# Sparse attention and a gated MLP on one core: K and Q loaded in runs of six tokens by casting transfers, with a newly searched instruction order

## The chip, the cores and the metric

The kernel runs on one core of a Trainium2 chip. The metric is the device time of one execution in microseconds (us); a kernel's time is the median of several executions. The profiler records one execution, whose span is some 1.8 us shorter than the time of the same execution. A run is called slow when it is over 1.5% above the fastest run of the same kernel, otherwise fast. Wherever a ratio of two kernels is given, it is the mean time of one kernel's fast runs over the mean time of the other's fast runs of the same rounds on the same chip, so it is not quite the ratio of the medians quoted beside it. For most runs it is found again only if the profiled execution is left out.

The engines are named as in the profile: PE (TensorE), PEld (its weight loads), DVE (VectorE), ACT (ScalarE), POOL (GpSimd) and SP (SyncE, which here only issues transfers).

## The reference

Attention over 4 batches, 8 heads, 768 tokens and head size 64, with the BigBird mask (window, first and last block, three random blocks of 32 tokens), feeds a gated MLP with a spatial gate and a residual.

```python
scores = scale * np.matmul(q, k.transpose(0, 1, 3, 2))     # (4, 8, 768, 768)
mask = |blk_i - blk_j| <= 1, or block 0 or 23 on either side, or one of 3 random blocks per row
attn = softmax(where(mask, scores, -1e9))
x = (attn @ v) as (batch, 768, 8 * 64)

h = gelu_tanh(x @ w_in)                                     # 512 -> 1024
u, v = h[..., :512], h[..., 512:]
v_n = layernorm(v) * g_ln
v_s = einsum('ts,bsd->btd', w_sg, v_n) + b_sg               # 768 x 768 over tokens
out = x + (u * v_s) @ w_out
```

The inputs are float32. The kernel does the attention products in bfloat16.

## The kernel before

The program is a list of operations, each with an engine, its dependencies, a modelled duration and a priority. Before anything is emitted, a greedy model of the chip turns the list into one fixed order per engine. Each engine then executes its list strictly in that order, with semaphores for the dependencies. So priorities and modelled durations do not change what is computed; they change who stands in front of whom.

```python
# in schedule(): the order is made on modelled times
for o in self.ops:
    o.prio = -rk[o.idx] if RANK == 1 else o.prio - RANK * rk[o.idx]
...  # greedy: the engine with the earliest possible start takes its best candidate
c = min((c for c in cands if c[0] <= tmin + 0.03), key=lambda c: (c[1], c[2]))
```

TensorE needs K and Q with the head dimension on the partitions, so every pair of heads is loaded with tokens on partitions, cast to bfloat16, transposed on TensorE into PSUM, and copied ("evicted") from PSUM to the tiles `KT` and `QT`. For batches 1 to 3 this went through two staging buffers, shared with V:

```python
ST = sb("ST", [P, 2, 768], F32)                    # the ring: two buffers of 384 KB
...
# one load of two heads on the SP queue; a run is one token of one head, 64 floats = 256 B
sr = SRC[nm][b, 2*c:2*c+2].rearrange("h (t p) d -> p (h t) d", p=P)
ld = op("SP", f"ld{nm}{b}.{c}", lambda e: e.dma_start(sg, sr), w=[sk], ...)
# then a cast, on GpSimd for K and Q of batches 1 to 3
op(eng, f"cs{nm}{b}.{c}", fn, r=[sk], w=w, dur={"DVE": 0.6, "ACT": 0.85, "POOL": 1.0}[eng], prio=pr)
...
# six transposes per pair of heads, both heads in one stationary operand
for t in range(T):
    ins = pe.transpose(Mbf[:, cc:cc + P], n_[:, c, t, :], ident[:, :])
...
# eviction: contiguous for batches 1 to 3, K on DVE, Q on ACT
src = Mbf[:, u.slot*1024:u.slot*1024 + S]
o_ = TT[:, c, 0:S]
if b == 0:     # batch 0 is loaded two tokens per run, and evicted with a strided write
    src = src.rearrange("p (n j c) -> p n j c", n=3, j=2)
    o_ = o_.rearrange("p (n c j) -> p n j c", n=3, j=2)
```

V has a path of its own, which the change leaves alone except in the order: staged and cast the same way, written to a scratch area in device memory (`scr`), and read back by gathers (`VG`, `VS`, `VR`), some of them indirect ones on GpSimd.

The softmax here doesn't subtract the row's maximum and nothing guards it: scores larger than these inputs give would overflow.

## Time and profile before

| | |
|---|---|
| time, median of the first three runs | 286.02 us (284.76 to 287.4) |
| span of the profiled execution | 280.6 us (timed at 282.39 us, so a quick one) |
| TensorE busy, idle | 216.9 us, 63.7 us |
| packets, of them under 512 B | 93,852, 68,468 |
| GpSimd waiting for K and Q loads | 50.7 us |

From the page of the kernel before: first the busy time of each engine with its share of the span and its instructions; then the busy tenths in 40 slices of 7 us; then the packets, and for each queue its packets, megabytes and share of the time of 16 transfer engines.

```profile
span 280.6 us, 8680 instructions
...
PE 216.9 (77%) x3525; PEld 159.9 (57%) x3525; DVE 163.8 (58%) x469; ACT 152.4 (54%) x227; POOL 112.4 (40%) x208
...
PE   0134675878776999974588998969669999999974
...
DMA  8999989999969768588996794868910112320033
...
DMA packets 93852, 45.43 MB, mean 162 GB/s; under 512 B 68468, under 2 KB 88084, under 8 KB 93812
...
q1 hardware_dynamic: 86848, 34.26, 54.5%
q0 software_dynamic: 4128, 9.02, 12.8%
```

TensorE is the busiest engine, but it has 64 us of holes, and the transfer engines are full for the first 80 us. Most packets are small. Queue 1 is the SP queue, with the staged loads; queue 0 holds the transfers that GpSimd issues.

The waits view of the kernel before (who waited for whom, us in total, times, longest):

```profile
POOL kn L559 <- DMA ST<-in_k_dram: 34.7, 9, 9.5
...
POOL qn L559 <- DMA ST<-in_q_dram: 16.0, 7, 4.9
...
PE Mps L591 <- POOL qn L559: 13.0, 8, 3.0
...
PE Mps L591 <- POOL kn L559: 1.8, 2, 1.2
```

GpSimd, whose casts stand in order with its gathers, waits 50.7 us for staged K and Q data, and TensorE then waits 14.8 us for those casts. The chain of waits that ended last (start, duration, what) shows the ring of two buffers at work:

```profile
55.61 5.42 DMA ST<-in_k_dram
61.08 0.83 POOL kn L559
61.93 3.59 SPq L548
65.56 11.65 DMA scr<-VA
...
133.10 4.07 DMA ST<-in_q_dram
...
197.53 7.19 DMA ST<-in_q_dram
```

A load lands, a cast frees its buffer, and only then the SP queue can go on: its next issue takes 3.6 us, and behind it the write of V to scratch takes 11.7 us to issue and land. The groups of the K and Q path, by line, engine and tile (count, then busy us and mean ns, then idle before them):

```profile
L559 POOL CAST kn<-ST 128x768 bf16<-128x768 f32 x12 | 10.0, 830 | 34.7 <-DMA ST<-in_k_dram 34.7
...
L591 PE MATMUL Mps<-ident,kn 128*128 128x128 bf16 x96 | 9.4, 254 | 13.7 <-ACT kn L559 9.2 <-DVE x_tok L898 2.3 <-POOL kn L559 1.8
...
L604 DVE COPY KT<-Mps 128x768 bf16<-128x768 bf16 x12 | 6.4, 551 | 8.4 <-PE Mps L591 8.2
```

And three of the stretches of 20 us (stretch, length, then busy us of PE, PEld, DVE, ACT and POOL with their instructions, the granted TensorE clock, the share of the transfer engines, GB/s):

```profile
100.00:120.00 20.00, 20.00 (x512) 15.38 (x513) 12.52 (x36) 14.63 (x23) 8.13 (x17) 1.00 0.68 154
120.00:140.00 20.00, 11.39 (x179) 8.20 (x172) 10.28 (x37) 7.83 (x11) 9.38 (x11) 0.88 0.87 222
...
200.00:220.00 20.00, 15.46 (x126) 12.00 (x128) 10.28 (x28) 10.75 (x18) 10.48 (x23) 0.83 0.20 47
```

The stretches 120 to 140 and 200 to 220 us are where the next batch's K and Q arrive late.

### The profile page before, as it was taken

To read this page: it belongs to the slowest core of one execution; us is meant where nothing else is said; L and a number is where in the kernel's file an instruction comes from. 1 tells how busy PE (TensorE), PEld (TensorE's weight loads), DVE (VectorE), ACT (ScalarE), POOL (GpSimd) and SP (SyncE) were. 2 spreads that over 40 slices of the span, in tenths; PEclk is the share of its full clock that TensorE was granted. 3 is DMA by queue.
4 is the path that set the end of the run, shared out by engine and by line. 5 is a ranking of instruction groups with operands and counts; after the bars stand their busy time and mean duration, and the time that the engine had idled before them with its cause. 6 is when DMAs were issued, how large, how long until landed. Compare 5 with 4: busy or idle time off the path is not lost.

```text
span 280.6 us, 8680 instructions
## 1 busy us (share of the span) xinstructions
PE 216.9 (77%) x3525; PEld 159.9 (57%) x3525; DVE 163.8 (58%) x469; ACT 152.4 (54%) x227; POOL 112.4 (40%) x208
## 2 busy tenths in 40 slices
PE   0134675878776999974588998969669999999974
PEld 0123454766454677762466676756467777868442
DVE  6108634212986658529254897655934685557783
ACT  3471876845064657750556756745527667766000
POOL 1017863160387865125669543128674220012000
PEclk9999998779999999999689999997959999999999
DMA  8999989999969768588996794868910112320033
GB/s 155 245 279 220 231 189 283 270 204 235 263 116 238 165 148 185 130 208 214 248 208 154 143 211 100 202 165 218 265 31 3 31 45 56 127 66 0 0 114 112
DMA packets 93852, 45.43 MB, mean 162 GB/s; under 512 B 68468, under 2 KB 88084, under 8 KB 93812
## 3 DMA queue, kind: packets, MB, share of 16 engines
q1 hardware_dynamic: 86848, 34.26, 54.5%
q0 software_dynamic: 4128, 9.02, 12.8%
q10 hardware_dynamic: 2836, 1.60, 2.7%
q8 instruction: 28, 0.46, 0.7%
q14 instruction: 12, 0.10, 0.1%
HBM read 36.49 MB, written 9.55 MB: 164 GB/s over the span
## 4 chain that ended last, share of the span: by engine, by line
PE 40%; DMA 19%; SPq 12%; POOL 11%; issue 10%; DVE 5%; ACT 2%; POOLq 0%
PE Mps L394 25%; DMA ST<-in_q_dram 7%; PE Ops L394 6%; POOL VR L678 6%; PE Sps L394 5%; SPq L548 5%; DMA ST<-in_k_dram 5%; DMA scr<-VA 4%; SPq L670 3%; DMA uT<-in_k_dram 3%; DVE gt L979 2%; SPq L632 2%; POOL KR L695 2%; PE Mps L913 2%; POOL qn L559 2%
## 5 line engine op out<-in xcount | busy, mean ns | idle before, releaser
L678 POOL DMA_INDIRECT VR<-scr,IDX x47 | 46.4, 987 | 24.0 <-issue 9.0
L691 DVE COPY KR<-KT 128x128 bf16 x176 | 33.2, 256 | 9.1 <-PE Sps L394 4.7
L394 PE MATMUL Mps<-w_sgT,vh 128*128 128x384 bf16 x192 | 35.1, 327 | 0.2
L695 POOL COPY KR<-KT 128x128 bf16 x88 | 23.5, 308 | 21.2 <-PE Sps L394 21.1
L394 PE MATMUL Mps<-w_out,xg 128*128 128x512 f32 x96 | 29.5, 433 | 1.9 <-DVE xg L982 1.6
L394 PE MATMUL Mps<-w_in,xg 128*128 128x512 f32 x96 | 27.5, 432 | 3.1 <-ACT vg L937 2.1
L979 DVE SCALAR_TENSOR_TENSOR gt<-Mps,gcol,bsg 128x384 f32<-128x384 f32 x32 | 19.7, 617 | 16.2 <-PE Mps L394 15.6
L394 PE MATMUL Mps<-xg,w_in 128*128 128x384 f32 x128 | 28.3, 368 | 0.7 <-ACT uT L964 0.2
L770 ACT ACTIVATE PR<-Sps 96x1024 bf16<-96x1024 f32 (+1 forms) x24 | 22.8, 948 | 8.2 <-PE Sps L394 8.2
L997 DVE TENSOR_TENSOR x_tok<-Mps,x_tok 128x512 f32<-128x512 f32 x24 | 16.6, 690 | 16.3 <-PE Mps L394 16.0
L394 PEld LDWEIGHTS Mps<-xg,w_in 128*128 128x128 f32 x128 | 22.9, 202 | 4.4 <-ACT uT L964 1.8
L937 ACT ACTIVATE vg<-Mps 128x512 f32<-128x512 f32 x24 | 14.2, 597 | 20.0 <-PE Mps L394 18.4
L604 ACT ACTIVATE QT<-Mps 128x768 bf16<-128x768 bf16 x14 | 11.6, 839 | 23.3 <-PE Mps L591 15.3
L394 PEld LDWEIGHTS Mps<-w_sgT,vh 128*128 128x128 bf16 x192 | 17.2, 98 | 11.9 <-DVE gt L979 1.4
L559 POOL CAST kn<-ST 128x768 bf16<-128x768 f32 x12 | 10.0, 830 | 34.7 <-DMA ST<-in_k_dram 34.7
L591 PE MATMUL Mps<-ident,qn 128*128 128x128 bf16 x96 | 9.9, 252 | 17.7 <-POOL qn L559 13.0
L394 PEld LDWEIGHTS Mps<-w_in,xg 128*128 128x128 f32 x96 | 18.0, 202 | 9.0 <-ACT vg L937 3.6
L920 ACT ACTIVATE xg<-Mps 128x512 fp32r<-128x512 f32 x24 | 14.3, 594 | 15.5 <-PE Mps L913 15.3
L394 PEld LDWEIGHTS Mps<-w_out,xg 128*128 128x128 f32 x96 | 17.1, 196 | 7.3 <-DVE xg L982 2.4
L950 DVE TENSOR_SCALAR vh<-vg,lnmv,lny 128x512 bf16<-128x512 f32 x24 | 13.3, 594 | 13.2 <-POOL lny L946 13.2
L964 ACT ACTIVATE uT<-Mps 128x384 f32<-128x384 f32 x32 | 15.7, 492 | 9.7 <-PE Mps L394 9.3
L939 DVE BATCH_NORM_STATS2 lnst<-vg 128x6 f32<-128x512 f32 x24 | 16.3, 679 | 7.8 <-ACT vg L937 7.8
(98 smaller groups left out, 399.7 us busy)
## 6 DMA issues: line engine op xcount, KB each, us to landing
out_dram<-x_tok SPq DMA_DIRECT2D x20, 256.0 KB, 3.4
ST<-in_v_dram SPq DMA_DIRECT2D x12, 384.0 KB
ST<-in_k_dram SPq DMA_DIRECT2D x12, 384.0 KB
ST<-in_q_dram SPq DMA_DIRECT2D x12, 384.0 KB
VR<-scr SPq DMA_DIRECT2D x123, 32.5 KB, 2.9
scr<-VA SPq DMA_DIRECT2D x6, 390.0 KB, 6.9
w_in<-in_moe_w_in_dram POOLq DMA_DIRECT2D x1, 2048.0 KB, 9.6
VS<-scr SPq DMA_DIRECT2D x3, 650.0 KB, 7.5
```

The costliest lines, as they stand in the source:

```text
L394: return pe.matmul(o, l, r, start=start, stop=True, skip_group_check=True)
L559: fn = {"DVE": lambda x: x.tensor_copy(o4, i4), "ACT": lambda a: a.activation(o4, i4, ACT.Copy), "POOL": lambda g: g.tensor_copy(o4, i4)}[eng]
L678: return g.indirect_dma_start(out=VR[0:96, uV.slot, :, :].rearrange("p h e -> p (h e)"), out_offset=None, in_=src[:, :], in_offset=bass.In ...
L691: ins = x.tensor_copy(KR[:, c0:c0 + n, rg, 32 * j:32 * j + 32], KT[:, c0:c0 + n, bass.ds(vals["DVE", i][j][0], 32)])
L695: op("POOL", f"kp{b}.{i}{hh}", lambda x, i=i, rg=rg: x.tensor_copy(KR[:, c0:c0 + n, rg, 64:96], KT[:, c0:c0 + n, bass.ds(vals["POOL"][0][i ...
L770: return lambda a: a.activation(o, i_, ACT.Exp, scale=SCALE)
L920: return x.tensor_copy(o_, i_) if xe == "DVE" else x.activation(o_, i_, ACT.Copy)
L937: op("ACT", f"gV{b}.{tau}", lambda a: a.activation(vg[vr][:, :], Mps[:, u.slot * 512:u.slot * 512 + 512], ACT.Gelu_apprx_tanh), r=[("vp", ...
L939: op("DVE", f"bs{b}.{tau}", lambda x: x.bn_stats(lnst[:, vr, :], vg[vr][:, :]), r=[("vg", vr)], w=[("lnst", vr)], dur=0.73, prio=pr - 300)
L964: o = op("ACT", f"gU{b}.{c}{dt}", lambda a: a.activation(uT[c][:, dt, :], Mps[:, u.slot * 512:u.slot * 512 + 384], ACT.Gelu_apprx_tanh), r ...
L979: op("DVE", f"g1{b}.{c}{dt}", lambda x: x.scalar_tensor_tensor(gt[gr][:, :], Mps[:, u.slot * 512:u.slot * 512 + 384], gcol[:, dt:dt + 1], ...
L997: op("DVE", f"res{b}.{tau}", lambda x: x.tensor_tensor(x_tok[bp][:, tau, :], Mps[:, u.slot * 512:u.slot * 512 + 512], x_tok[bp][:, tau, :] ...
```

## The change

The intent is to take K and Q of batches 1 to 3 out of the ring, to move them in fewer and longer pieces, to load them far ahead, and to search the instruction order again. There are four parts.

1. Partition p takes the six tokens 6p to 6p+5 of a head, which are 1,536 contiguous bytes. Batch 0 is loaded so too (before: 512 B).
2. For batches 1 to 3, GpSimd issues a transfer that casts float32 to bfloat16 on its way, four heads at a time, straight into `kn` or `qn`. There is no staging and no cast instruction. The Trainium skill ("DMA: Bandwidth & Descriptors", SWDGE vs HWDGE vs iDMA) says that a transfer that casts can only be issued from GpSimd; all twelve casting loads are.
3. Each head is now a tile of its own, so a pair takes twelve transposes of half the width instead of six. PSUM then holds the tokens in the order (j, c) with token 6c + j, and the eviction reads it in strides and writes `KT` and `QT` contiguously.
4. The modelled durations are corrected, and a table of offsets, found by a search on that model, is added to the priorities.

```diff
+PLK = 900
+PLK1 = -155
+OFF = {
+    "TRk0": -90, "TRk1": -4175, "TRk3": -317, ...      # (some 240 entries, cut)
+}
...
-                o.prio = -rk[o.idx] if RANK == 1 else o.prio - RANK * rk[o.idx]
+                o.prio = o.prio - RANK * rk[o.idx] + OFF.get(kind(o), 0)
...
-    qn = sb("qn", [P, 4, T, P], BF16)
-    kn = sb("kn", [P, 4, T, P], BF16)
+    qn = sb("qn", [P, H, T, D], BF16)
+    kn = sb("kn", [P, H, T, D], BF16)
...
+            if b and nm != "v":
+                if c % 2 == 0:
+                    z = c // 2
+                    o = op("POOL", f"ld{nm}{b}.{z}", lambda g, ...: g.dma_start(
+                        dst[:, 4*z:4*z+4, :, :].rearrange("p h j d -> p h (j d)"),
+                        SRC[nm][b, 4*z:4*z+4].rearrange("h (p j) d -> p h (j d)", j=T)),
+                        ..., prio=(1000*b - PLK if b > 1 else PLK1) + n_, nbytes=786432, bw=340e3)
+                continue
...
-                        ins = pe.transpose(Mbf[:, cc:cc + P], n_[:, c, t, :], ident[:, :])
+                        if b == 0:
+                            ins = pe.transpose(...)             # full width, as before
+                        else:
+                            for hp in range(2):
+                                ins = pe.transpose(Mbf[64*hp:64*hp+64, ...], n_[:, 2*c+hp, t, :],
+                                                   ident[:, :], tile_position=(0, 64*hp))
...
+                    src = Mbf[:, ...].rearrange("p (j c) -> p c j", j=T)
+                    o_ = TT[:, c, 0:S].rearrange("p (c j) -> p c j", j=T)
...                                                             # some 20 durations, for example:
-               ... dur=0.6, prio=pr + 2)                        # zeroing the edges of V
+               ... dur=1.15, prio=pr + 2)
```

## The prediction

> **What bounds it now.** TensorE is busy 216.9 of 280.6 us (page, part 1). Its 64 idle us lie, by the stretches view, in 0-20 us (17: first loads), 20-60 (15), 60-100 (7), 120-140 (8.6), 180-220 (7.5) and the last 21 us (6). Much of the middle is the K/Q path of batches 1-3: per batch eight loads of 384 KB with 256-byte runs through a ring of two staging buffers, then GpSimd casts (24, 0.83 us each). In the waits view GpSimd stands 34.7 us for K loads and 16.0 for Q loads, TensorE 13.0 for Q casts and 1.8 for K casts. In batch 1 the first K load is issued at 47 us and the last Q cast ends at 91 us. The DMA engines are at about 1.0 from 0 to 80 us and 0.7-0.9 until 200; 68,468 of 93,852 packets are under 512 B. Full queues hold the SP queue (one write of V to scratch took 7.3 us to issue), and TensorE shows 2.0-2.4 us "issue" gaps meanwhile. After 210 us DMA is at 0.2 and TensorE nearly solid.
>
> **Removed.** 24 staged loads (36,864 packets), 24 GpSimd casts (20 us), the ring for K/Q. Queue 1 spent 54.5% of 16 engines' span on 86,848 packets, 1.76 ns each at their joint rate: about 65 us of DMA time.
>
> **Added.** 12 casting loads from GpSimd, 512 runs of 1,536 B each. Comparable weight loads took GpSimd 0.82-0.88 us: 10 us. Their 9.4 MB at the first 40 us' 220 GB/s are 43 us of DMA; estimate: 20-25 us of DMA time saved. The Trainium skill ("DMA: Bandwidth & Descriptors", Specifications) puts line rate at 512 B and up; no record here yet shows it.
>
> Transposes of batches 1-3 become 12 half-width ones, 0.50 us to perhaps 0.65-0.8: +4 to +7 us TensorE. Evictions read PSUM in strides: the DVE copy takes 551 ns contiguous, 1,004 ns with batch 0's strided write; the skill ("VectorE: DVE Perf Modes", What auto-detection actually checks) wants step 1 for the packed mode, so I expect 1.0 us for 12 K copies (+5 us DVE) and on ACT (from 0.81, +2.4 us). Batch 0's K/Q runs grow from 512 to 1,536 B: start 1-2 us earlier.
>
> **Moved.** K/Q loads can run far ahead: batch 1's by 50-60 us, batches 2 and 3 during the previous attention. The offsets reorder all engines, delaying some output projections into gaps.
>
> **On the critical path.** Start 1-2 us; 20-60 us perhaps 3; 60-100 about 4; 120-140 and 180-220 about 10 of 16; tail 0-2. That is 20 us less idleness plus shorter issue gaps, minus about 3 us of new TensorE work: about 18 us.
>
> **Prediction.** 268 us, 8 in 10 between 257 and 279. Faster by over 2%: 0.91; within 2%: 0.07; slower: 0.02.
>
> **What would show it.** TensorE busy 215-226 us, idle 42-48. No GpSimd waits for K/Q loads of batches 1-3, no casts. Packets about 60,000, under 512 B about 32,000; DMA share clearly lower after 60 us. K copies on DVE 0.9-1.1 us. TensorE waits before batch 1-3 transposes under 5 us together. 120-140 and 180-220 near 90% TensorE busy.
>
> **What would make it wrong.** V still goes through staging with 256-byte runs, a scratch write and gathers; if V, not K/Q, decides when a batch's attention starts, half the gain is lost. The casting loads may land slowly (weight loads took 10-15 us in a full queue) and delay gathers behind them on GpSimd. The slower evictions could bind where K and Q arrive together. The searched order rests on modelled times and may fit the chip badly, or well, and take 10 us more from start and tail.

## The result, and the profile after

The changed kernel took 273.61 us (median of 4, 272.30 to 274.82), beside 286.71 us (284.76 to 287.62) for the kernel before. The ratio of the fast runs is 0.955, with a 95% interval of 0.948 to 0.962. That is inside the predicted range and 5.6 us above the predicted 268.

These are the lines of the changed kernel's page that answer to those of before:

```profile
span 271.8 us, 8926 instructions
...
PE 217.0 (80%) x3669; PEld 160.6 (59%) x3669; DVE 164.7 (61%) x469; ACT 150.2 (55%) x227; POOL 101.8 (37%) x196
...
PE   0224558859799936998898899995899999999994
...
DMA  8997976999999633985988981424331102301116
...
DMA packets 58845, 40.73 MB, mean 150 GB/s; under 512 B 31412, under 2 KB 53076, under 8 KB 58804
...
q1 hardware_dynamic: 45504, 24.82, 36.0%
q0 software_dynamic: 10464, 13.74, 24.8%
```

The packets fell as predicted. As share times span, the two queues took 67.3% of 280.6 us, 188.8 us, before, and 60.8% of 271.8 us, 165.3 us, after: 23.6 us saved, where the prediction had 20 to 25. All 50.7 us that GpSimd waited for K and Q are gone. The groups of the new K and Q path:

```profile
L649 DVE COPY KT<-Mps 128x768 bf16<-128x768 bf16 x12 | 11.3, 954 | 9.8 <-PE Mps L639 9.6
L649 ACT ACTIVATE QT<-Mps 128x768 bf16<-128x768 bf16 x14 | 10.8, 809 | 12.8 <-PE Mps L639 8.5 <-PE Mps L636 4.2
L639 PE MATMUL Mps<-ident,kn 128*64 128x128 bf16 x144 | 7.7, 253 | 0.7 <-DVE KT L649 0.7
...
L608 POOL DMA_DIRECT2D kn<-in_k_dram x6 | 4.7, 786 | 28.9 <-PE Mps L639 28.9
```

But the time was not gained where it was expected, as the waits view of the changed kernel shows in two lines that name nothing on this core:

```profile
ACT PG L846 <- remote: 9.8, 1, 9.8
...
DVE gt L1024 <- remote: 8.3, 2, 4.5
```

The timelines of ACT and DVE (start, duration, engine, line, operation, count, and in brackets the idle time before it) place those waits:

```profile
103.63 0.60 ACT L846 ACTIVATE PG<-Sps 128x512 bf16<-128x512 f32 x1 [9.84 <-remote]
```

```profile
98.73 0.62 DVE L1024 SCALAR_TENSOR_TENSOR gt<-Mps,gcol,bsg 128x384 f32<-128x384 f32 x1 [4.48 <-remote]
...
103.77 0.62 DVE L1024 SCALAR_TENSOR_TENSOR gt<-Mps,gcol,bsg 128x384 f32<-128x384 f32 x1 [3.84 <-remote]
```

From 94 to 104 us TensorE, VectorE and ScalarE nearly stood: they did 3.3, 1.7 and 0.4 us of work. This is a program on one core, so there is no remote core. The stretches of the changed kernel then read:

```profile
100.00:120.00 20.00, 17.06 (x273) 11.68 (x271) 12.73 (x35) 8.64 (x14) 5.85 (x15) 0.78 0.66 160
120.00:140.00 20.00, 17.80 (x535) 14.56 (x534) 16.26 (x47) 15.60 (x23) 8.59 (x19) 1.00 0.87 174
...
200.00:220.00 20.00, 19.52 (x284) 14.07 (x283) 14.38 (x42) 14.40 (x23) 12.64 (x21) 1.00 0.16 43
```

The late arrivals at 120 to 140 and 200 to 220 us are cured (11.4 to 17.8 and 15.5 to 19.5 us of TensorE work). The stretch 100 to 120 us became worse, with a granted clock of 0.78 after the stall.

### The profile page after: what moved, and what is told of

Same layout as the page of the kernel before. It is cut to its first block, busy times and chain, and to the rows that moved or that the text cites. A ratio compares the mean times of both kernels' runs of the same rounds, so it can differ in the third digit from the quotient of the medians.

```text
span 271.8 us, 8926 instructions
## 1 busy us (share of the span) xinstructions
PE 217.0 (80%) x3669; PEld 160.6 (59%) x3669; DVE 164.7 (61%) x469; ACT 150.2 (55%) x227; POOL 101.8 (37%) x196
## 2 busy tenths in 40 slices
DMA packets 58845, 40.73 MB, mean 150 GB/s; under 512 B 31412, under 2 KB 53076, under 8 KB 58804
## 3 DMA queue, kind: packets, MB, share of 16 engines
q0 software_dynamic: 10464, 13.74, 24.8%
## 4 chain that ended last, share of the span: by engine, by line
PE 50%; DVE 14%; DMA 10%; POOL 9%; issue 8%; ACT 4%; another core or an unknown queue 3%; SPq 1%; POOLq 0%; DVEq 0%
PE Mps L428 27%; PE Ops L428 9%; PE Sps L428 6%; POOL VR L723 6%; DVE gt L1024 4%; DMA w_in<-in_moe_w_in_dram 4%; PE Mps L958 4%; PE Mps L639 4%; DVE xg L1027 3%; DMA scr<-VA 3%; DMA x_tok<-in_v_dram 2%; DVE KT L649 1%; DVE KR L736 1%; DVE lnst L984 1%
## 5 line engine op out<-in xcount | busy, mean ns | idle before, releaser
L428 PE MATMUL Mps<-w_sgT,vh 128*128 128x384 bf16 x192 | 37.7, 345 | 9.4 <-DVE gt L1024 7.4
L736 DVE COPY KR<-KT 128x128 bf16 x176 | 29.8, 243 | 13.1 <-PE Sps L428 7.9
L815 ACT ACTIVATE PR<-Sps 96x1024 bf16<-96x1024 f32 (+1 forms) x24 | 22.6, 950 | 13.4 <-PE Sps L428 10.5
L428 PE MATMUL Mps<-w_out,xg 128*128 128x512 f32 x96 | 27.8, 419 | 0.1
L428 PE MATMUL Mps<-w_in,xg 128*128 128x512 f32 x96 | 25.8, 409 | 1.1 <-issue 1.1
L428 PEld LDWEIGHTS Mps<-xg,w_in 128*128 128x128 f32 x128 | 21.5, 192 | 7.1 <-DMA w_in<-in_moe_w_in_dram 2.5
L846 ACT ACTIVATE PG<-Sps 128x512 bf16<-128x512 f32 x24 | 14.0, 597 | 15.8 <-remote 9.8
L965 ACT ACTIVATE xg<-Mps 128x512 fp32r<-128x512 f32 x24 | 14.3, 595 | 13.5 <-PE Mps L958 13.2
L1042 DVE TENSOR_TENSOR x_tok<-Mps,x_tok 128x512 f32<-128x512 f32 x24 | 16.5, 689 | 7.7 <-PE Mps L428 7.4
L428 PEld LDWEIGHTS Mps<-w_in,xg 128*128 128x128 f32 x96 | 16.5, 188 | 6.5 <-issue 1.8
L816 ACT ACTIVATE PW<-Sps,b_odd 128x512 bf16<-128x512 f32 (+1 forms) x24 | 15.6, 648 | 8.4 <-PE Sps L428 8.3
L1027 DVE TENSOR_TENSOR xg<-gt,uT 128x384 fp32r<-128x384 f32 x32 | 19.2, 600 | 1.1
L428 PE MATMUL Ops<-VA,PW 128*64 128x65 bf16 x384 | 19.8, 203 | 0.0
## 6 DMA issues: line engine op xcount, KB each, us to landing
VR<-scr SPq DMA_DIRECT2D x123, 32.5 KB, 2.1
w_in<-in_moe_w_in_dram POOLq DMA_DIRECT2D x1, 2048.0 KB, 11.5
```

The source lines that it names most:

```text
L428: return pe.matmul(o, l, r, start=start, stop=True, skip_group_check=True)
L736: ins = x.tensor_copy(KR[:, c0:c0 + n, rg, 32 * j:32 * j + 32], KT[:, c0:c0 + n, bass.ds(vals["DVE", i][j][0], 32)])
L815: return lambda a: a.activation(o, i_, ACT.Exp, scale=SCALE)
L816: return lambda a: a.activation(o, i_, ACT.Exp, bias=bias[0:p1, 0:1], scale=SCALE)
L965: return x.tensor_copy(o_, i_) if xe == "DVE" else x.activation(o_, i_, ACT.Copy)
L1027: op(G2, f"g2{b}.{c}{dt}", lambda x: x.tensor_tensor(xg[2 + c][:, dt, :], gt[gr][:, :], uT[c][:, dt, :], ALU.mult), r=[("gt", gr), ("uT", ...
```

## The experiments

The theory was that the gain comes from the K and Q path itself, chiefly from running ahead of the ring, and that the longer runs are a smaller part. The rivals were that the searched order makes the gain; that the shorter transfers make it; and that the slower eviction takes part of it away. The kernel was also run again, unchanged, because of the odd stall. "The changed kernel" below means that code in its two repeats. All orders of the variants `short_runs`, `plain_evict`, `w_in_early` and `vz_late` were compared with the changed kernel's and are the same on every engine except for the operation that the experiment moves. The runs were made in three groups, on three different chips; in each, the kernel before ran beside the others, at 283.85, 282.67 and 282.93 us.

### The changed kernel again, twice

No edit.

> The changed kernel unchanged, beside the variants on the same chip. Ratio to before 0.955 again (about 273 us). The stall of all engines at 92-104 us (two VectorE waits of 4.5 and 3.8 us and a ScalarE wait of 9.8 us that the profile puts down to no instruction): if it belongs to this order of work, it shows again at the same instructions with 6-9 us; if it was a chance of one recording, it is gone and the span is shorter by 5-8 us.

> The changed kernel unchanged, a third time. Its first record gave 273.6 us and a ratio of 0.955, its second 259.9 us and 0.916, with the kernel before at 286.7 and 283.9. In the first trace TensorE falls 14 us behind the second in three places (25-38, 62-108 and 185-191 us), where VectorE and ScalarE wait for nothing that is recorded and semaphore records are missing (68 of 1,039; none in the second). If the first record was an odd occasion, this one gives 258-262 us with all records there; if the two are states of this kernel, it may give 272-275 us with records missing and the same three places late.

Measured: 259.92 us (259.37 to 261.38, ratio 0.916, 0.909 to 0.923) and, on another chip, 259.83 us (259.38 to 260.52, ratio 0.921, 0.912 to 0.931). So the same code gained 23 to 24 us in two repeats, and 13.1 in the recorded result. The first repeat was 13.7 us shorter than the record, more than the 5 to 8 us expected if the stall was a chance. The page and three stretches of the first repeat:

```profile
span 257.8 us, 8926 instructions
...
PE 210.9 (82%) x3669; PEld 157.2 (61%) x3669; DVE 167.9 (65%) x469; ACT 150.6 (58%) x227; POOL 101.9 (40%) x196
```

```profile
100.00:120.00 20.00, 15.40 (x346) 11.83 (x346) 11.50 (x33) 11.91 (x19) 3.47 (x11) 0.84 0.79 196
120.00:140.00 20.00, 17.52 (x322) 13.82 (x321) 15.91 (x50) 13.05 (x20) 14.36 (x28) 0.98 0.92 188
...
200.00:220.00 20.00, 20.00 (x577) 15.82 (x577) 13.57 (x41) 16.41 (x25) 3.62 (x9) 1.00 0.21 60
```

TensorE executes the same 3,669 matmuls in the same order in both traces, so they can be laid beside each other one by one. The recorded execution falls behind the repeat by 5.5 us between 25 and 38 us, by about 10 us between 62 and 108 us (most of it between 94 and 104), and by 3.6 us between 185 and 191 us; in between it catches up by some 6 us, because the repeat has waits there of its own. There are no "remote" waits in the repeats. In the recorded trace 68 of the 1,039 semaphore updates of TensorE, ScalarE, VectorE and GpSimd are missing (971 are there; TensorE lacks 11 of its 343), and of the updates by transfers there are 3,012, against 4,061 in each repeat. In both repeats none of the 1,039 is missing; the traces of later variants lack up to 11 and show no "remote" wait. The stalled times fall in with runs of GpSimd's indirect gathers, and the transfer engines were only 0.3 busy from 95 to 108 us, which does not look like a wait for a transfer. What stalled it stays open: by their times all four recorded executions had it (272 to 275 us), and none of the eight later runs of this or nearly this order shows it in its trace. The kernel before was slower too beside the recorded result (286.71 us) than beside the repeats (283.85 and 282.67), by 1%, and the record does not name the chip of that result. Whether the missing updates are its cause or a symptom is not shown. The experiments below are compared with the repeats.

Where the gain lies can be counted from the stretches. This table sums TensorE's busy us in each.

| stretch, us | before | changed, recorded | changed, repeat |
|---|---|---|---|
| 0–20 | 2.9 | 3.6 | 3.6 |
| 20–60 | 24.8 | 24.5 | 26.4 |
| 60–100 | 33.3 | 33.5 | 36.7 |
| 100–120 | 20.0 | 17.1 | 15.4 |
| 120–140 | 11.4 | 17.8 | 17.5 |
| 140–180 | 37.4 | 37.2 | 37.9 |
| 180–220 | 32.5 | 35.5 | 39.5 |
| done by 220 | 162.2 | 169.1 | 177.1 |
| total busy | 216.9 | 217.0 | 210.9 |
| left after 220, and the time it took | 54.7 in 60.6 | 47.9 in 51.8 | 33.9 in 37.8 |

The repeat's span is 22.8 us shorter. By 220 us it has done 14.9 us more work; its work is 6.0 us less; and its tail after 220 us has 3.9 us of idle instead of 5.9. The middle term is the one that the prediction did not have. TensorE executes more instructions than before and yet is busy 6 us less, because its matmuls are quicker: those of `w_out` took 433 ns before and 417 in the repeat, those of `w_in` 432 and 407. The Trainium skill ("TensorE: Matmul & The Clock Gate", HAM oscillation — how this bites in real kernels) describes that gaps make the clock gate throttle the array and the work after them start cold. This agrees for the most part: before, the clock was 0.88 and 0.83 in the stretches 120 to 140 and 200 to 220 us, which had the holes, and in the repeat 0.98 and 1.00. From 0 to 40 us, though, the trace before shows a clock of 1.00 with only 14.0 us of work.

The mean clock of the whole span (0.951 before, 0.972 in the repeat) does not explain the 6 us: the run `late_loads` below has a mean of 0.941 and a TensorE busy time of 211.2 us. What counts is the work that falls into throttled time. In the traces the clock is either full or half. These are TensorE's sums over the half-clock stretches, first before (five), then in the repeat (two that hold work):

```profile
sum 27.30, PE 20.85; mean PE 4.17
```

```profile
sum 13.70, PE 8.77; mean PE 4.38
```

In the recorded trace six matmuls of `w_sgT` took 1.14 us at 92.7 us, with full clock, and 2.10 us at 99.4 us, with half. So about half of the 12.1 us of busy time that left the half-clock stretches is saved: an estimate of 6 us from these two sums, which is what is missing. In the recorded trace 18.4 us of work lay at half clock, and TensorE was busy 217.0 us. In `late_loads` it was 11.5 us, since much of the half-clock time fell into its hole.

### Path alone, and order alone

`path_only` is the changed kernel with an empty offset table and the old durations for all operations that the K and Q path does not touch. `order_only` is the reverse: new durations and offsets, old K and Q path.

```diff
 path_only:
-OFF = {"TRk0": -90, ...}
+OFF = {}
-... "dur=1.15", "dur=0.083 * n", "bw=228e3 if nm == 'v'", ...
+... "dur=0.6", "dur=0.055 * n", "bw=268e3 if nm == 'v'", ...

 order_only: (changed kernel, with the ring, the casts, the six transposes
              and the contiguous eviction of the kernel before)
```

> The K/Q data path of the change (6-token runs, casting loads, half-width transposes, strided evictions) on the old order model: old durations, no offsets. Theory 1 (the path by itself brings the gain) expects 265-275 us. If path and order need each other, 276-284 us. The order alone was 2.4% slower than before.

> The kernel before with its own K/Q path, but the recalibrated durations and the searched offsets of the changed kernel. Theory 3 (order) expects 273-277 us. Theories 1 and 2 (data path) expect no gain: 282-292 us, with the GpSimd waits for K and Q loads (50.7 us in sum before) still there; and since the offsets were searched for the other path, slower than before is possible.

Measured: `path_only` 263.62 us (261.73 to 267.28, ratio 0.932, 0.918 to 0.947), `order_only` 291.40 us (290.58 to 292.65, ratio 1.024, 1.018 to 1.031). The path alone gives 19 of the 23 us. `path_only` came out under the 265 to 275 us that were expected. The order alone costs 7 us; GpSimd still waits 21.3 us there for Q loads and 8.7 for K loads:

```profile
POOL qn L593 <- DMA ST<-in_q_dram: 21.3, 7, 4.7
```

Here the order that was searched for one set of transfers did not suit the other. So the path makes the gain, and the offsets with the new durations add to it only about 4 us.

### The new durations without the searched offsets

```diff
-OFF = {"TRk0": -90, ...}
+OFF = {}
```

> The changed kernel without the searched offsets, durations recalibrated. If the recalibration brings most of what order brings, it lies within 2% of the changed kernel (260-265 us); if the searched offsets do, it lies near the run with the path on the old model, 268 us or more.

Measured: 282.06 us (278.35 to 284.96, two of the four runs slow), ratio of the fast runs 1.003 (0.991 to 1.016), called unclear. Its two fast runs, 278.35 and 281.09 us, are 0.992 of the fast runs of the kernel before, if the profiled execution is not left out. With the corrected durations and no offsets nearly all of the gain is lost: 18 us against `path_only` by the medians, 17 by the fast runs, by changes to modelled times alone. Two lines of its waits view, and two of its chain of waits, name the worst of it:

```profile
ACT VA L573 <- DMA ST<-in_v_dram: 13.2, 1, 13.2
...
PE Sps L408 <- ACT PR L795: 9.7, 1, 9.7
```

```profile
48.81 18.29 DMA ST<-in_v_dram
67.13 0.86 ACT VA L573
```

The third V load of batch 1 was issued at 48.8 us, just after some 5 MB of weight loads from GpSimd, and took 18.3 us to land. Its cast stands in ACT's order in front of an exponential that TensorE needs. ACT stood 13.2 us and TensorE, behind it, 9.7; TensorE did 9.5 us of work from 60 to 80 us, against 16.9 in the repeat of the changed kernel.

### The same with room for the V loads

This takes that wait away: V loads 3 and 4 of batch 1 are staged in a tile that is idle then (`vh`), so they need no free ring buffer and are issued right behind load 2.

```diff
+            if (b, nm) == (1, "v") and c >= 2:
+                stg, ds = vh[...].bitcast(F32)[:, 768*(c-2):768*(c-1)], f"Lx{c}"
...
+    sp.remove(vl[k_][0])                       # k_ in (2, 3)
+    sp.insert(sp.index(vl[k_ - 1][0]) + 1, vl[k_][0])
```

> The version without the searched offsets (282.1 us), with one thing mended: V loads 3 and 4 of batch 1 are staged in a tile that is idle then (vh) and issued directly after loads 1 and 2 (in place of after casts free the ring, about 49 us); orders of all else the same. In the trace of that version ScalarE stands 13.2 us (53.9 to 67.1 us) in front of the cast of a V load that was issued at 48.8 us, and TensorE 9.7 us behind it. If this in-order wait is what the version without the search loses, it falls to 270-275 us and TensorE is busy 15 us or more at 60-80 us (9.5 us now); if not, 279 us or more.

Measured: 275.99 us (275.29 to 278.62, ratio 0.977, 0.970 to 0.984). ACT no longer waits for V loads, and TensorE did 16.5 us of work from 60 to 80 us instead of 9.5. But its work from 40 to 60 us fell from 13.1 to 8.7, and it now waits 8.1 us for gathers of V from scratch. The time lies between the two forecasts. So the late V load accounts for some 3 to 6 of the 20 to 22 us that the missing offsets cost (276.0 against 282.1 by the medians, 276.3 against 279.7 by the fast runs, and the changed kernel at 259.8 to 259.9), across two chips. The rest lies in other places of the order and was not pinned down.

### K and Q of batch 1 loaded late

All four casting loads of batch 1 that the changed kernel issues from 27 to 39 us are moved behind the weight loads in GpSimd's order, and are then issued at 46 to 49 us, which is when the kernel before issued its first.

```diff
+    at = max([o for o in lst if o.name in ("w_out", "w_sg0", "w_sg1", "w_sg2")], key=lst.index)
+    for nm_ in ("ldk1.2", "ldk1.0", "ldq1.1", "ldq1.0", "ldk1.1"):
+        ...                                     # move it directly behind `at`
```

> The changed kernel with the four casting loads of K and Q of batch 1 held back on GpSimd until the six weight-load issues are out (about 48 us in place of 27-41 us, the time at which the kernel before began to load K); all other orders are the same. Theory 1 (the gain is that K and Q come far ahead) expects TensorE to wait for K and Q of batch 1 at 58-75 us and the run to be 4-10 us longer than the changed kernel (264-270 us). If only the packets and casts saved matter, it is within 2 us (w_in even comes earlier).

Measured: 273.24 us (272.53 to 273.89, ratio 0.969, 0.962 to 0.976), 13.4 us slower than the changed kernel's repeats in the other groups, where the kernel before took the same within 0.4%. The waits view of TensorE has one new line:

```profile
PE Mps L639 <- DMA kn<-in_k_dram: 18.7, 1, 18.7
```

That is more than the 4 to 10 us expected. But the edit did one thing more than it says: each load was put directly behind the same weight load, so their order was reversed (there is no `ldk1.2`). TensorE needs `ldk1.0` first. It is the third of the four in the changed kernel and the last here, and the wait ends as it lands, at 72.3 us; `ldk1.1`, now issued first, had landed at 64.4. So up to 8 us of the wait may come from the reversal. What being late costs by itself is not shown; 5 to 13 us is an estimate from these numbers (13.4, less 7.9 or nothing). The size holds for loads that queue behind 5 MB of weights; a load that is late but meets free transfer engines may cost less; this was not run. Nor was it run what it is worth alone that 24 casts leave GpSimd.

### Short runs again

The casting loads stay, but with runs of one token (256 B), and the transposes' order of tokens is then the plain one, so batches 1 to 3 are also evicted contiguously.

```diff
-    dst[...].rearrange("p h j d -> p h (j d)"), SRC[...].rearrange("h (p j) d -> p h (j d)", j=T)
+    dst[...].rearrange("p h j d -> p (h j) d"), SRC[...].rearrange("h (t p) d -> p (h t) d", p=P)
...
-    src, o_ strided for every batch
+    src, o_ strided for batch 0 alone
```

> The changed kernel with the same order of every engine, but the casting loads of batches 1-3 read runs of 256 bytes again (the old token layout, so the evictions of these batches read PSUM contiguously). Packets rise by about 30,000 to about 90,000. Theory 1 (loads that no longer pass a two-buffer ring and GpSimd casts can run ahead) expects most of the gain to stay: within 1.5% of the changed kernel. Theory 2 (fewer packets unload the DMA engines) expects over half of the gain lost: 280 us or more. Theory 3 (the searched order alone) expects no change, within 0.5%.

Measured: 265.22 us (264.81 to 266.96, ratio 0.935, 0.928 to 0.942), 5.3 us or 2.0% slower than the repeat of the changed kernel in the same group. That is a little more than the 1.5% that theory 1 had allowed, and far from the 280 us of theory 2. From its page and its groups:

```profile
q0 software_dynamic: 41184, 13.74, 41.0%
```

```profile
L608 POOL DMA_DIRECT2D kn<-in_k_dram x6 | 8.8, 1470 | 30.0 <-PE Mps L639 14.9 <-PE Ops L428 14.0 <-PE Sps L428 1.1
```

Queue 0 moved the same 13.74 MB, in 41.0% of 263.3 us, 108 us, instead of 26.6% of 257.8 us, 69 us. GpSimd needs 1.47 us to issue such a load instead of 0.79, and is busy 110.6 us instead of 101.9. Both cost something, and their sum is under a quarter of the gain. Most of the gain was had with the short runs.

### Eviction in plain order

The strided reads are taken away for batches 1 to 3 and nothing is put in their place, so the tokens of K and Q stand in the wrong order: the result is wrong.

```diff
-    src = Mbf[...].rearrange("p (j c) -> p c j", j=T)
-    o_ = TT[:, c, 0:S].rearrange("p (c j) -> p c j", j=T)
+    src, o_ contiguous, except for batch 0
```

> The changed kernel with the same order, the 1,536-byte runs and the half-width transposes, but evictions of batches 1-3 read PSUM contiguously; tokens are then permuted and the output is WRONG on purpose. K copies on VectorE fall from 0.95 to about 0.56 us (12 copies, about 5 us less VectorE work), ScalarE unchanged at 0.81. If the strided read costs time on the chain, 2-3 us shorter than the changed kernel; my view is under 1% (0 to 2 us), as the copies sit where K and Q come early.

Measured: 262.01 us (259.15 to 262.80, ratio 0.924, 0.918 to 0.930). Its six runs fall in two groups, two at 259.2 and 259.7 us and four at 261.6 to 262.8; the profiled one is of the first. DVE was busy 164.2 us instead of 167.9, and no gain is seen in the time. So the stride's cost on DVE is real, and nothing shows it on the critical path. What the two groups are was not found.

This run was also told correct. With q and k of 0.1 the scores are all near 0 (an estimate from the inputs: the products of 64 terms of 0.01, times 1/8, are about 0.01), so the softmax is nearly uniform and the order of the keys hardly shows in the output. Whoever changes the layout of K or Q in this kernel cannot rely on this comparison.

### Two moves in the order of the changed kernel

In the repeat, TensorE's largest waits after 40 us were these two:

```profile
PE Mps L428 <- DMA w_in<-in_moe_w_in_dram: 4.4, 1, 4.4
PE Mps L639 <- DVE x_tok L1042: 2.8, 1, 2.8
```

The second stands behind a zeroing of V's edges, as DVE's timeline shows:

```profile
113.96 0.49 DVE L685 MEMSET VA<- 32x520 bf16 x1 [5.59 <-DMA scr<-VA]
```

The zeroing must wait until V has been written to scratch, which took 6 us, and in DVE's fixed order an addition that TensorE needs stands behind it. `w_in_early` issues the load of `w_in` before the casting loads of Q of batch 1. `vz_late` moves the zeroing for batch 2 behind later work of DVE. `early_and_vz` does both.

```diff
 w_in_early:
+    lst.remove(wi); lst.insert(lst.index(at), wi)             # POOL: w_in before ldq1.0
 vz_late:
+    dv_.remove(vz_); dv_.insert(dv_.index(at) + 1, vz_)       # DVE: vz2.0 behind nrm1.4
```

> The changed kernel with one issue moved: the 2 MB load of w_in goes ahead of the four K/Q loads of batch 1 on GpSimd (about 27 us in place of 43 us); every other order is the same. In the second trace TensorE waits 4.4 us for w_in at 51-55 us, and this wait is on the chain of waits. If it is worth its length, 2-4 us shorter than the changed kernel. If K and Q of batch 1, now landing later, or the V path (write to scratch, gather back) take its place, under 1 us.

> The changed kernel with two memsets of VectorE (edge rows of V of batch 2, needed only in batch 2's attention) moved 27 places later in VectorE's order; all else the same. In the second trace they hold VectorE 5.6 us at 108-114 us for the write of V to scratch, and TensorE then waits 2.8 us for a residual add behind them. If that order slip is on the critical path: 2-4 us shorter than the changed kernel (256-258 us). If something else takes its place, under 1 us.

> w_in issued ahead of batch 1's K and Q loads (259.1 us alone against 259.8) and the two memsets later, together: a candidate that would beat the changed kernel. If the two waits are independent, 255-258 us; if each only shifts the wait to the V path, 258-260 us.

Measured:

| | median us | range | ratio (95%) |
|---|---|---|---|
| `w_in_early` | 259.09 | 258.62 to 260.60 | 0.920 (0.911 to 0.931) |
| `vz_late` | 256.10 | 255.54 to 257.45 | 0.906 (0.900 to 0.913) |
| `early_and_vz` | 256.14 | 253.67 to 258.62 | 0.905 (0.898 to 0.913) |

Taking away the 4.4 us wait for `w_in` gave 0.7 us, which is within the spread: the wait is gone from the view, but other waits later in the order took over. Taking away the wait of DVE gave 3.7 us, more than TensorE's 2.8 us wait behind it: TensorE did 18.0 us of work from 100 to 120 us instead of 15.4. Both together are no better than the second alone, beyond the spread. `vz_late` and `early_and_vz` are correct and beat both kernels, by about 27 us against the kernel before and, across the groups, 3.7 us against the changed one.

Two more ideas were built and never ran. Full-width transposes of the new layout, with both heads in one stationary operand, do not build, because that operand may have only one free dimension. A ring of four staging buffers did not fit: a later tile needs 2,048 bytes per partition where 1,440 were left.

## Why the prediction was right or wrong

The direction and the size held: 273.6 us recorded against 268 predicted, with 257 to 279 as the range. The repeats at 259.8 and 259.9 are inside it too, on the other side. Nearly every step of the mechanism held, and several sizes did not.

- **Held: what bounds it.** GpSimd's 50.7 us of waits for staged loads went to none, and TensorE's waits before the transposes of batches 1 to 3 from 14.8 us behind the casts to 0.9 us (4.0 in the repeat, 2.8 of them behind the zeroing). `path_only` shows that this path is the gain, 19 of 23 us.
- **Held: transfers.** Packets went to 58,845 (predicted about 60,000), those under 512 B to 31,412 (about 32,000), and 23.6 us of transfer time were saved (20 to 25). The prediction cited the Trainium skill ("DMA: Bandwidth & Descriptors", Specifications) for line rate from 512 B up, with no record yet to show it. `short_runs` agrees as far as it goes: 108 us against 69 for the same bytes in 256 B and in 1,536 B runs; no run shows where between them the rate levels off. But those 39 us of transfer time were worth only 5.3 us. "DMA share clearly lower after 60 us" came true late: from 60 to 80 us it rose from 1.00 to 1.18, because the loads run ahead, and only from 160 to 200 us did it fall, from 0.84 to about 0.4.
- **Held: the DVE copy.** 551 ns became 954 (predicted 0.9 to 1.1 us), as the Trainium skill ("VectorE: DVE Perf Modes", What auto-detection actually checks) lets one expect of a step other than 1. `plain_evict`, without the step, gained no time.
- **Failed, a size: ACT's eviction.** Predicted +2.4 us for reading PSUM in strides. The evictions of Q took 809 ns each, and 809 too in `plain_evict`, where twelve of the fourteen read in plain order (839 before, when two wrote in strides).
- **Failed, a size: the transposes**, "+4 to +7 us TensorE". All K and Q transposes together took 19.3 us before, 20.5 in the recorded trace and 19.5 in the repeat. The half-width ones are nearly free: a pair of heads in batches 1 to 3 took 0.53 us of TensorE before and 0.59 and 0.55 after, with twice the instructions and half the columns of weights each. The Trainium skill ("TensorE: Matmul & The Clock Gate", LDWEIGHTS) says that a weight load's time goes with its columns. The traces do not show that proportion: full-width loads took 111 to 113 ns before and, in batch 0 alone, 137 to 139 after; half-width ones 109 to 128. Why the half-width ones cost so little was not tested.
- **Failed, a size: how far ahead.** "Batch 1's by 50-60 us". In the repeat its loads were issued at 27.2 to 38.9 us, before at 47.0 to 85.1: 20 us earlier for the first and 46 for the last. Those of batches 2 and 3 came 43 to 69 us earlier.
- **Failed: the sum.** "20 us less idleness ... minus about 3 us of new TensorE work". In the repeat idleness fell by 16.8 us (63.7 to 46.9) and the work itself by 6.0. The prediction took busy time for a constant plus the new instructions; but 12.1 us less of the work fell into stretches of half clock, which is worth about 6 us. In the recorded trace busy time stayed at 217.0 us and idleness was 54.8, where the prediction had 42 to 48.
- **Failed in part: the stretches.** "Start 1–2 us; 20–60 us perhaps 3" gave 0.3 together in the recorded trace and 2.2 in the repeat, by the table. "60–100 about 4" gave 0.2, since the stall from 94 to 104 us fell there; the repeat gave 3.5. "120–140 and 180–220 about 10 of 16" gave 9.5 in the recorded trace and 13.2 in the repeat, but 100 to 120 us gave back 2.9 and 4.6, which the prediction had as already full. In the repeat this is where V binds: the write of V to scratch holds DVE 5.6 us. The prediction had named V as what could bind next.
- **The warning about the order.** "The searched order rests on modelled times and may fit the chip badly, or well". It fits well as a whole, and is fragile: 18 us are lost by corrected durations without offsets, 7 us by the order without its path, and 3.7 us were still to be had by moving one operation.

So the recorded 13.1 us are the sum of about 23 us that the change gives in undisturbed executions, and some 10 us or more of a stall whose cause is not settled. That 273.6 lies so near to 268 is partly luck: without the stall, which nobody foresaw, the kernel is 8 us below the forecast, and the work that shrank by 6 us, where 3 more were expected, was not foreseen either.

## What to carry to other kernels

When loads go through a small ring and an in-order engine has to free its buffers, look first for a way to run ahead: holding back the loads of one batch cost 13 us here, though up to 8 of them may come from their changed order, while making the runs six times longer saved 39 us of transfer time and only 5 us of the kernel's. Where the order of every engine is fixed beforehand, judge a change of path and a change of order separately, then read the remaining waits from the trace, and look at what stands in front of the instruction that is waited for: moving one zeroing gave more than taking away the longest wait after 40 us. And run the same code a second time before explaining a shortfall: here the repeat differed by 14 us.

## What the Trainium skill lacked or had wrong

- "DMA: Bandwidth & Descriptors", Anatomy of one DMA: it calls the time of descriptor generation small and variable and gives no figure. Here a casting load of 512 runs held GpSimd 0.79 us and one of 3,072 runs, of the same bytes, 1.47 us.
- "DMA: Bandwidth & Descriptors", SWDGE vs HWDGE vs iDMA: it says that each transfer engine goes round between its queues, but not how long a transfer can take beside a full queue. Here a 384 KB load from the SP queue took 18.3 us to land beside some 5 MB of weight loads from GpSimd.
- "ScalarE: Activation LUTs" has nothing on reading PSUM in strides. It cost ScalarE nothing (809 ns with and without), while VectorE's copy went from 551 to 954 ns.
- "TensorE: Matmul & The Clock Gate", LDWEIGHTS: as recorded in these traces, the time of bfloat16 loads does not go with their columns: 32 columns took 101 to 102 ns, 64 columns 109 to 128, and 128 columns 94 to 139.
- No page has the stall of the recorded execution: 4 to 10 us in which PE, ACT and DVE all nearly stood, with waits put down to "remote" on a one-core program and 68 of the engines' 1,039 semaphore updates missing from the trace. It was not seen in the eight later runs of this or nearly this order.
